# One written order for all engine queues, with batch 0's k and the whole of w_out loaded earlier

## The chip, the cores and the metric

The kernel runs on one core of one Trainium2 chip. The number given is device time in microseconds (us) of one execution; the reported time of a kernel is the median of its runs. The core has a matrix engine (PE, with its weight loads shown apart as PEld), a vector engine (DVE), an activation engine (ACT), a general engine (POOL), and a queue engine (SP) which here only issues transfers. POOL issues transfers too, and in the kernel before ACT issues one. Each engine works through its own queue strictly in program order; engines wait for each other by semaphores.

## The reference

Linear attention over 8 batches of 8 heads (576 positions, head size 64), and behind it a gated network without a nonlinearity:

```python
q_s = exp(q - max(q, axis=-1)); q_s = q_s / (sum(q_s, axis=-1) + 1e-9)   # over the 64 of a head
k_s = exp(k - max(k, axis=2));  k_s = k_s / (sum(k_s, axis=2) + 1e-9)    # over the 576 positions
kv  = einsum('bhsd,bhse->bhde', k_s, v)
attn = einsum('bhsd,bhde->bhse', q_s, kv)
x = attn.transpose(0, 2, 1, 3).reshape(4608, 512)
out = ((x @ w1) * (x @ w2)) @ w3 @ w_out        # w1, w2: 512x1024; w3: 1024x1024; w_out: 1024x512
```

All inputs and the output are float32. q, k and v have 1152 KB per batch each, w1, w2 and w_out 2 MB each, w3 4 MB: 38.8 MB are read.

## The kernel before, in words

The kernel is one class, `Plan` (L18), and one function. The function doesn't emit instructions as it goes: it registers **steps** with `plan.add` (L50): a name, an engine (or a choice of two, settled by the table `PICKS`, L206), an estimated length, a closure that emits the instructions, the steps it needs, and the ring of buffers that it takes from. At the end `plan.run` (L154) emits all 773 steps in one sequence, and that sequence is the order of every engine's queue. Before, `order` (L87) finds the sequence by list scheduling: it keeps a clock for each engine, takes the engine with the earliest start, and on it the ready step of highest worth, which is the longest path behind it (`tails`, L67) plus a lead from a table (`LEADS`, L166). For transfers it counts one bus of 409 GB/s.

The names, by stage:

- **Loads** (`load`, L396; table `LOADS`, L241). `q.0.1` is the second part of q of batch 0 (positions 4 to 8 of each group of 9; 640 KB), `q.0.0` the first (512 KB); `k.b`, `v.b`, `q.b` a whole batch. `w3.0` to `w3.3` are one row block of w3 each (512 KB of float32), `w3.4` and `w3.5` two (1 MB); `wo.0`, `wo.1` the halves of w_out (1 MB each); `w1.i`, `w2.i` column quarters (512 KB). Weights, and v of batches 0 and 1, are cast to float16 by the transfer. The weights and the first batches go through POOL's queue, at most eight in flight: the ninth waits for the first (the `slot` in L424). `q.0.1` is issued by SP, `q.0.0` by ACT. From `q.2` on loads go through SP, which starts on them once `LOADS[-3]` (L425) has landed.
- **Fold** (`fold`, L430): w3 and w_out are multiplied once into `W3O`. For each of 8 row blocks `ft`: `w3t.ft`, 8 transposes on PE (L434); `w3T.ft`, the copy out; `pf.ft.0` and `pf.ft.1`, 4 matmuls each (L444), which need `wo.0` and `wo.1`; `W3O.ft`, the scaled copy.
- **Attention** of batch b (L460): `qmx`, `qsub`, `qexp`, `qsm`, `qeps`, `qrc`, `qn` are the softmax of q (max, subtract, exp, sum, epsilon, reciprocal, product), for two parts `.0` and `.1`; `kmx`, `cb`, `ksub`, `kexp` the column maximum of k, its spread over partitions, subtract, exp; `vc` the cast of v from batch 2 on; `kv` (L555, L564) and `kv2` the product of k and v and its scaling; `qt`/`qT` the transposes of q for batches 0 and 1 on PE, and `qd` (L643) those of later batches as DMA transposes issued by SP; `xm`, `xt` (L661) the product with q and `xs`, `xts` its scaled copies.
- **Network** of chunk c (L772; 512 tokens of batch c, and a ninth chunk of the remainders): `up.1` and `up.0` (L786) with w2 and w1, `bs` the copy of the first, `ab` the product of the two on DVE (L801), `down.c.tb` with `W3O` (L808, in the last chunk L823), `os` the copy out, `st` the store.

PSUM rings hold 4 buffers for `up` and `w3t`, 2 for `down` and `pf`, 2 for the attention's products. Steps of POOL and DVE that read two tensors from SBUF (`port`, L159) are chained to one another by explicit waits in the early part, so that the two engines take turns.

Ahead of the first real matmul, 24 matmuls of zeros run on PE (`WARM`, L329, L363 to L368).

Of the kernel before, what the change touches and what calls it, by code (L numbers as in the profile page):

```python
# [10 lines left out]
F32 = mybir.dt.float32  # L11
# [6 lines left out]
class Plan:  # L18


    RATE = 409.0e3
    LAND = 1.7
    HOP = 0.15
    NEAR = 0.2
    LINKED = 50.0
    BUS = 2.2
    BEGIN = {"SP": 0.74, "POOL": 1.25, "DVE": 1.0, "ACT": 0.74, "PE": 1.0}

    def __init__(self, rings, leads, picks):
        self.rings = rings  # L30
        self.leads = leads
        self.picks = picks
        self.steps = {}

    @staticmethod
    def key(name):


        if name[0] == "up":
            return f"up{name[1]}_{min(name[2], 3)}"  # L40
        if len(name) > 2 and name[1] < 2 and name[0] not in ("bs", "ab", "down", "os", "st", "pf"):
            return "_".join(str(x) for x in name)
        return f"{name[0]}_{min(name[1], 3) if len(name) > 1 else 0}"

    @staticmethod
    def group(name):

        return f"{name[0]}_{min(name[1], 3)}_" + "_".join(str(x) for x in name[2:])
# [18 lines left out]
    def tails(self, users):  # L67
        tail = {}
        for first in self.steps:
            stack = [first]  # L70
            while stack:
                n = stack[-1]
                if n in tail:
                    stack.pop()
                    continue
                todo = [u for u, _ in users.get(n, ()) if u not in tail]
                if todo:
                    stack += todo
                    continue
                s = self.steps[n]  # L80
                own = s["length"] + (self.LAND + s["size"] / self.RATE if s["size"] else self.HOP)
                tail[n] = own + max([tail[u] if whole else tail[u] - own
                                     for u, whole in users.get(n, ())], default=0.0)
                stack.pop()
        return tail

    def order(self):  # L87
        steps = self.steps
        free = dict(self.BEGIN)
        ends = {}  # L90
        fifo = {tag: [] for tag in self.rings}
        given = {}
        users = {}
        for s in steps.values():
            for taken in s["gives"]:
                given.setdefault(taken, []).append(s["name"])
            s["open"] = len(s["needs"]) + len(s["after"])
            s["at"] = 0.0
            for n in s["needs"]:
                users.setdefault(n, []).append((s["name"], True))  # L100
            for n in s["after"]:
                users.setdefault(n, []).append((s["name"], False))
        tail = self.tails(users)
        for rank, n in enumerate(sorted(steps, key=str)):
            steps[n]["rank"] = -rank
        for s in steps.values():
            s["worth"] = tail[s["name"]] + s["lead"] + self.leads.get(self.key(s["name"]), 0.0)
        ready = [s for s in steps.values() if not s["open"]]
        bus = self.BUS
        port, holder = -9.0, None  # L110
        order = []
        while ready:
            could = {}
            for s in ready:
                at = max(free.get(s["eng"], 0.0), s["at"])
                if s["port"]:
                    at = max(at, port + (self.HOP if holder != s["eng"] else 0.0))
                if s["takes"]:
                    ring = fifo[s["takes"]]
                    last = [n for old in range(len(ring) - self.rings[s["takes"]],  # L120
                                               len(ring) - self.rings[s["takes"]] + s["slots"])
                            if old >= 0 for n in given.get(ring[old], ())]
                    if any(n not in ends for n in last):
                        continue
                    at = max([at] + [ends[n] + self.HOP for n in last])
                could.setdefault(s["eng"], []).append((at, s))
            assert could, "the plan is stuck"
            eng = min(sorted(could), key=lambda e: min(at for at, _ in could[e]))
            soon = min(at for at, _ in could[eng]) + self.NEAR
            at, s = max(((at, s) for at, s in could[eng] if at <= soon),  # L130
                        key=lambda c: (math.floor((c[1]["worth"] - c[0]) * 1e6 + 0.5), c[1]["rank"]))
            ready.remove(s)
            if s["takes"]:
                fifo[s["takes"]] += [s["name"]] * s["slots"]
            free[eng] = at + s["length"]
            if s["port"]:
                port, holder = at + s["length"], s["eng"]
            end = at + s["length"]
# [788 lines left out]
```

## Time and profile before

| | |
|---|---|
| median of 3 runs | 245.75 us (245.39, 245.75, 275.76) |
| the profiled execution | 246.01 us, of it 244.2 us from the first to the last instruction (the span) |
| PE busy | 234.2 us (96%) |
| DVE / ACT / POOL busy | 177.1 / 123.8 / 118.9 us |
| mean granted clock of PE | 0.993 |
| read / written | 38.80 MB / 9.44 MB |

The profile page gives busy times, the span in 40 slices, the chain of work that ended last, and groups of instructions with the idle time before them. The trace answers for a stretch of time with the instructions of an engine in order (the timeline), with who waited for whom (the waits) and with busy time and granted clock (the windows). A step can be found in it by its line and its tiles: L444 `po<-wosb,w3T` with four matmuls is one `pf`.

### The profile page before, as it was taken

Reading aid. Unit: us, or ns where it says so; the run is one execution under the profiler, and the core shown is the slowest. Engines: PE = TensorE matmul, PEld = TensorE weight load, DVE = VectorE, ACT = ScalarE, POOL = GpSimd, SP = SyncE. Lnnn points to the kernel's source line nnn. Section 1 sums busy time; section 2 is a strip of 40 time slices with the busy share of each in tenths; the row PEclk is TensorE's granted clock in tenths of the full one; section 3 lists DMA queues with packets and bytes.
Section 4 is the critical chain, followed back from the end, with each engine's and each line's share of the span. In section 5 each row is a group of like instructions: output and inputs, shape, how many; then the busy total and the mean of one; then the engine's idle time right before and its main releaser. Section 6 shows DMA issues by size and latency. Waiting matters only on the chain.

```text
span 244.2 us, 4819 instructions
## 1 busy us (share of the span) xinstructions
PE 234.2 (96%) x1908; PEld 114.8 (47%) x1908; DVE 177.1 (73%) x303; ACT 123.8 (51%) x189; POOL 118.9 (49%) x76
## 2 busy tenths in 40 slices
PE   7868999999999799999999999999999999999994
PEld 2435644556758244344444444444444344444443
DVE  0889789787998889998998899799965115573210
ACT  0556686466687357575565566555443612202221
POOL 8357769678880577086666646864470000000000
PEclk9979999999999999999999999999999999999999
DMA  7999999999999854986997299700840115000343
GB/s 206 267 253 252 305 300 200 249 369 387 392 399 209 215 120 148 397 190 76 348 313 148 51 364 319 160 4 6 183 83 3 43 43 132 0 0 0 86 132 129
DMA packets 37894, 45.66 MB, mean 187 GB/s; under 512 B 15984, under 2 KB 22384, under 8 KB 37872
## 3 DMA queue, kind: packets, MB, share of 16 engines
q1 hardware_dynamic: 29552, 33.69, 48.4%
q0 software_dynamic: 7792, 11.14, 20.7%
q10 hardware_dynamic: 528, 0.52, 0.6%
q8 instruction: 15, 0.25, 0.4%
q14 instruction: 7, 0.06, 0.1%
HBM read 38.80 MB, written 9.44 MB: 197 GB/s over the span
## 4 chain that ended last, share of the span: by engine, by line
PE 65%; DMA 21%; POOL 5%; DVE 4%; issue 2%; SPq 1%; ACT 1%; POOLq 0%; ACTq 0%
PE pab L786 40%; PE po L808 19%; DMA w<-in_moe_w_dram 6%; DMA w1sb<-in_moe_w_dram 5%; DMA v<-in_v_dram 4%; PE po L823 3%; DMA qT<-en 3%; DMA q<-in_q_dram 2%; POOL en L620 2%; POOL q L588 2%; PE xm L661 2%; PE pkv L555 1%; DVE q L588 1%; DVE qm L583 1%; DVE qr L601 1%
## 5 line engine op out<-in xcount | busy, mean ns | idle before, releaser
L801 DVE TENSOR_TENSOR ab<-pab,bsb 128x512 f16<-128x512 f32 x72 | 49.1, 686 | 28.7 <-PE pab L786 22.9
L786 PE MATMUL pab<-x,w2sb 128*128 128x512 f16 (+1 forms) x288 | 65.9, 356 | 0.0
L786 PE MATMUL pab<-x,w1sb 128*128 128x512 f16 (+1 forms) x288 | 65.9, 356 | 0.0
L808 PE MATMUL po<-W3O,ab 128*128 128x512 f16 x256 | 59.3, 380 | 0.0
L620 POOL TENSOR_TENSOR en<-eq,qr 128x1024 f16<-128x1024 f16 (+1 forms) x16 | 33.8, 2123 | 31.1 <-DVE qr L613 15.3
L342 ACT CAST bsb<-pab 128x512 f16<-128x512 f32 x42 | 24.5, 584 | 44.0 <-PE pab L786 34.6
L530 POOL TENSOR_TENSOR k<-k,cb 128x1152 f32<-128x1152 f32 x15 | 39.1, 2625 | 14.3 <-issue 7.1
L786 PEld LDWEIGHTS <-w2sb 128*128 128x128 f16 x320 | 30.6, 98 | 29.9 <-issue 0.2
L786 PEld LDWEIGHTS <-w1sb 128*128 128x128 f16 x320 | 30.7, 98 | 29.5 <-DMA w1sb<-in_moe_w_dram 0.2
L808 PEld LDWEIGHTS <-ab 128*128 128x128 f16 x256 | 23.9, 98 | 29.2 <-issue 2.9
L342 ACT COPY osb<-po 128x512 f32<-128x512 f32 (+1 forms) x33 | 19.1, 578 | 35.5 <-PE po L808 18.2
L588 POOL TENSOR_TENSOR q<-q,qm 128x1280 f32<-128x1280 f32 (+1 forms) x13 | 27.6, 2142 | 8.5 <-DVE qm L583 8.5
L342 DVE CAST bsb<-pab 128x512 f16<-128x512 f32 x30 | 20.4, 683 | 8.8 <-PE pab L786 7.8
L472 DVE TENSOR_REDUCE km<-k 128x128 f32<-128x1152 f32 x12 | 25.4, 2123 | 0.7 <-DMA k<-in_k_dram 0.7
L583 DVE TENSOR_REDUCE qm<-q 128x16 f32<-128x1024 f32 (+1 forms) x16 | 21.4, 1344 | 5.8 <-DMA q<-in_q_dram 5.8
L596 ACT ACTIVATE eq<-q 128x1024 f16<-128x1024 f32 (+1 forms) x16 | 18.6, 1164 | 7.3 <-POOL q L588 5.0
L601 DVE TENSOR_REDUCE qr<-eq 128x16 f32<-128x1024 f16 (+1 forms) x16 | 21.1, 1325 | 1.3 <-ACT eq L596 1.3
L538 ACT ACTIVATE ek<-k 128x1152 f16<-128x1152 f32 x16 | 18.6, 1165 | 5.9 <-POOL k L530 4.4
L346 ACT ACTIVATE x<-xm 128x512 f16<-128x512 f32 x29 | 16.2, 597 | 6.8 <-PE xm L661 6.7
L444 PE MATMUL po<-wosb,w3T 128*128 128x512 f16 x64 | 16.2, 394 | 3.0 <-ACT w3T L342 1.8
L342 ACT CAST v<-v 128x1152 f16<-128x1152 f32 x11 | 12.4, 1158 | 4.7 <-DMA v<-in_v_dram 4.7
L444 PEld LDWEIGHTS <-w3T 128*128 128x128 f16 x64 | 5.9, 100 | 10.0 <-ACT w3T L342 3.6
(62 smaller groups left out, 169.1 us busy)
## 6 DMA issues: line engine op xcount, KB each, us to landing
out_dram<-osb SPq DMA_DIRECT2D x66, 128.0 KB, 2.4
q<-in_q_dram SPq DMA_DIRECT2D x6, 1152.0 KB, 8.7
v<-in_v_dram SPq DMA_DIRECT2D x6, 1152.0 KB, 11.6
k<-in_k_dram SPq DMA_DIRECT2D x5, 1152.0 KB, 5.6
k<-in_k_dram POOLq DMA_DIRECT2D x3, 1152.0 KB, 11.9
v<-in_v_dram POOLq DMA_DIRECT2D x2, 576.0 KB, 14.6
w<-in_moe_w_dram POOLq DMA_DIRECT2D x2, 512.0 KB, 11.8
wosb<-in_moe_w_out_dram POOLq DMA_DIRECT2D x2, 512.0 KB, 11.8
```

The source lines that it names most:

```text
L342: return [(nc.scalar.copy if eng == "ACT" else engine[eng].tensor_copy)(out=out, in_=in_)]
L444: nc.tensor.matmul(st["pf", ft], lhsT=st["w3T", ft][:, gt, :], rhs=wosb[:, gt, :], start=(gt == 0), stop=(gt == N_FT - 1))
L472: dve.tensor_reduce(out=st["km", b][:, two(hp), :], in_=kb[:, two(hp), :, :].rearrange("p h j d -> p h d j"), axis=AX.X, op=ALU.max)
L530: return [engine[eng].tensor_tensor(out=kb[:, two(hp), :, :], in0=kb[:, two(hp), :, :], in1=st["cb", b][:, two(hp), None, :].broadcast_to( ...
L538: nc.scalar.activation(out=st["ek", b][:, hp, :, :].rearrange("p j (i d) -> p i j d", i=2), in_=kb[:, two(hp), :, :], func=AF.Exp)
L583: dve.tensor_reduce(out=st["qm", b][:, :, j], in_=qb[:, :, j, :], axis=AX.X, op=ALU.max)
L588: return [engine[eng].tensor_tensor(out=qb[:, :, j, :], in0=qb[:, :, j, :], in1=st["qm", b][:, :, j, None].broadcast_to([P, HH, n, D]), op ...
L601: dve.tensor_reduce(out=st["qr", b][:, :, slice(*PARTS[p])], in_=st["eq", b, p], axis=AX.X, op=ALU.add)
L620: return [engine[eng].tensor_tensor(out=st["en", b][:, j, :, :].rearrange("p j h d -> p h j d"), in0=st["eq", b, p], in1=st["qr", b][:, :, ...
L786: nc.tensor.matmul(st["p", one, c, sub, u][:, a * (t1 - t0):(a + 1) * (t1 - t0)], lhsT=w[:, ct, fb * P:(fb + 1) * P], rhs=x()[:, ct, t0:t1 ...
L801: dve.tensor_tensor(out=st["ab", c][:, nf * u:nf * u + nf, t0:t1], in0=cut(st["p", 0, c, sub, u]), in1=cut(st["bsb", c, sub, u]), op=ALU.mult)
L808: nc.tensor.matmul(st["po", c, tb], lhsT=st["ab", c][:, ft, tb * P:(tb + 1) * P], rhs=W3O[:, ft, :], start=(ft == 0), stop=(ft == N_FT - 1))
```

## The change

The list scheduler, its leads and its constants are removed. A string `ORDER` names all steps in sequence, and `run` emits them so, after asserting that each step's needs stand ahead of it. 76 steps move to another engine, nearly all by the table `PICKS`. Dead code goes (`PEMAX`, the 32-bit identity `ident32` on POOL); loads can be put on SP by a list `HW`, from which a path for uncast weights exists but is unused. In particular:

- `q.0.0` is issued by SP behind `q.0.1`, not by ACT.
- POOL's first loads come as w3.4, k.0, wo.0, wo.1, w3.3, w3.0, w3.1, where they were w3.4, wo.0, k.0, w3.3, wo.1, w3.0, w3.1; the identity is made ahead of w3.3, not behind q.1.0. Later, w3.2 is ahead of k.1 and w1.0 ahead of k.2.
- `LOADS[-3]`, which SP's `q.2` waits for, is now `w2.3`; before, it was `w1.3`.
- 17 zero matmuls at the start where there were 24, and 16 in the queue of PE right ahead of `pf.4.0`.
- The turn-taking waits cover the first 191 steps of the list; before, those planned for the first 50 us.
- The moves between engines: among them `qn.0.0` from POOL to DVE, `qsub.0.0` from DVE to POOL, the second `vc` of batches 2 to 7 from ACT to POOL, and 66 copies and epsilon steps (`bs`, `os`, `xs`, `xts`, `qT`, `W3O`, `w3T`, `qeps`) between ACT and DVE, in both directions.

PE's 243 steps are the same; their sequence differs in places. Up to `kv.0`, both sequences hold the same set. From `w3t.5` it now reads:

```text
w3t.5 w3t.4 (16 zeros) pf.4.0 pf.5.0 pf.4.1 qt.0.8 w3t.3 pf.5.1 qt.0.16 w3t.0 pf.3.0 pf.3.1 w3t.1
qt.0.0 pf.0.0 pf.1.0 pf.0.1 kv.0 ...
```

and before it was

```text
w3t.4 w3t.5 pf.4.0 pf.5.0 qt.0.0 w3t.3 pf.4.1 pf.5.1 w3t.0 qt.0.8 qt.0.16 pf.3.0 pf.3.1 w3t.1
pf.0.0 pf.0.1 pf.1.0 kv.0 ...
```

SP's queue around batch 2 is now `q.2 v.2 k.3 q.3 v.3 k.4 q.4 st.0.0 st.0.1 st.0.2 qd.2.1 qd.2.0 st.1.0 v.4`; before, `q.2 v.2 k.3 q.3 v.3 k.4 st.0.0 q.4 v.4 st.0.1 st.0.2 qd.2.1 qd.2.0`.

```diff
-    def order(self):
...
-        tail = self.tails(users)
...
-        return order, ends
-    def run(self, link):
-        held = None
-        for at, s in self.order()[0]:
+    def run(self, link, fill):
+        assert sorted(self.first, key=str) == sorted(self.steps, key=str)
...
+        for i, name in enumerate(self.first):
+            s = self.steps[name]
+            assert done.issuperset(s["needs"]) and done.issuperset(s["after"]), name
...
+            if ".".join(str(x) for x in name) in FILL:
+                fill(FILL[".".join(str(x) for x in name)])
             got = s["emit"]()
-            if s["port"] and at < self.LINKED:
+            if s["port"] and i < LINKED:
...
+LINKED = 191
+ORDER = """
+q.0.1 q.0.0 w3.4 k.0 wo.0 wo.1 ident w3.3 w3.0 qmx.0.1 w3.1 q.1.0 qsub.0.1 qexp.0.1 qmx.0.0 w3t.5
+v.0 w3t.4 qsm.0.1 w3T.4 qsub.0.0 qeps.0.1 w3.5 qexp.0.0 kmx.0.0 w3T.5 w3.2 pf.4.0 qrc.0.1 cb.0
+qn.0.1 pf.5.0 pf.4.1 qsm.0.0 k.1 qt.0.8 W3O.4 w2.0 w3t.3 qeps.0.0 ksub.0.1 pf.5.1 w3T.3 w1.0
+qt.0.16 w3t.0 qrc.0.0 qT.0.8 qn.0.0 pf.3.0 kexp.0.1 pf.3.1 w3T.0 ksub.0.0 w3t.1 W3O.5 qt.0.0
+w3T.1 W3O.3 pf.0.0 qmx.1.0 pf.1.0 kexp.0.0 qT.0.0 pf.0.1 qT.0.16 qsub.1.0 k.2 kv.0 w2.1 W3O.0
...
+ab.0.0.6 up.1.0.0.7 xs.1.0.1 ksub.2.1 xs.1.0.0 up.0.0.0.7 bs.0.0.7 qmx.1.1 kexp.2.0 up.1.1.0.0
+up.0.1.0.0 ab.0.0.7 qsub.1.1 kexp.2.1 up.1.1.0.1 qmx.2.1 bs.1.0.0 up.0.1.0.1 bs.1.0.1 ab.1.0.0
+down.0.0 qsub.2.1 qexp.1.1 qmx.2.0 vc.2.0 ab.1.0.1 q.3 up.1.1.0.2 v.3 qsm.1.1 vc.2.1 up.0.1.0.2
+k.4 qexp.2.1 up.1.1.0.3 qsub.2.0 os.0.0 qsm.2.1 up.0.1.0.3 qeps.1.1 bs.1.0.2 kv.2 qrc.1.1
+qexp.2.0 ab.1.0.2 down.0.1 qn.1.1 kv2.2 bs.1.0.3 q.4 st.0.0 ab.1.0.3 down.0.2 os.0.1 qmx.3.1
+st.0.1 qt.1.8 os.0.2 qeps.2.1 qrc.2.1 qt.1.16 qsub.3.1 down.0.3 qsm.2.0 qT.1.8 st.0.2 qT.1.16
+qmx.3.0 xm.1.1 down.1.0 xs.1.1.0 qn.2.1 kmx.3.1 xs.1.1.1 up.1.1.1.0 vc.3.0 qeps.2.0 up.0.1.1.0
+qexp.3.1 qd.2.1 qrc.2.0 kmx.3.0 qn.2.0 xt.1 up.1.1.1.1 os.0.3 up.0.1.1.1 bs.1.1.0 xts.1.0
+qsub.3.0 qd.2.0 up.1.1.1.2 xts.1.1 bs.1.1.1 qsm.3.1 ab.1.1.0 os.1.0 down.1.1 bs.1.1.2 ab.1.1.1
+st.1.0 up.0.1.1.2 os.1.1 qmx.4.1 up.1.1.1.3 v.4 st.1.1 ab.1.1.2 up.0.1.1.3 bs.1.1.3 qeps.3.1
+st.0.3 xm.2.0 vc.3.1 ab.1.1.3 down.1.2 xs.2.0.1 cb.3 xs.2.0.0 qsub.4.1 qexp.3.0 xm.2.1 down.1.3
...
+"""
+FILL = {
+    "begin": 17, "pf.4.0": 16,
 }
...
+HW = [
+    ("q", 0, 1), ("q", 0, 0),
+]
 LOADS = [
-    ("q", 0, 1), ("q", 0, 0), ("w3", 4), ("wo", 0), ("k", 0), ("w3", 3), ("wo", 1), ("w3", 0),
-    ("w3", 1), ("q", 1, 0), ("v", 0), ("w3", 5), ("k", 1), ("w3", 2), ("w2", 0), ("k", 2),
-    ("w1", 0), ("w2", 2), ("w2", 1), ("w1", 1), ("w1", 2), ("v", 1), ("w1", 3), ("w2", 3),
-    ("q", 1, 1),
+    ("w3", 4), ("k", 0), ("wo", 0), ("wo", 1), ("w3", 3), ("w3", 0), ("w3", 1), ("q", 1, 0),
+    ("v", 0), ("w3", 5), ("w3", 2), ("k", 1), ("w2", 0), ("w1", 0), ("k", 2), ("w2", 1),
+    ("w1", 1), ("w2", 2), ("w1", 2), ("v", 1), ("w2", 3), ("w1", 3), ("q", 1, 1),
 ]
...
-    if WARM:
-        zero = konst.tile([P, 512], F16)
-        dve.memset(zero, 0.0)
-        idle = p_att([P, 512], F32, "idle")
-        for i in range(WARM):
+    zero = konst.tile([P, 512], F16)
+    dve.memset(zero, 0.0)
+    def fill(n):
+        idle = p_o()
+        for i in range(n):
             nc.tensor.matmul(idle, lhsT=zero[:, 0:P], rhs=zero, start=True, stop=True)
+    if FILL.get("begin"):
+        fill(FILL["begin"])
...
-    loads = [(n, ("SP", "ACT")[i] if i < 2 and n[0] in ("q", "k") else "POOL")
-             for i, n in enumerate(LOADS)]
+    loads = [(n, "SP") for n in HW] + [(n, "POOL") for n in LOADS]
...
-    plan.run(link)
+    plan.run(link, fill)
```

## The prediction

> **What bounds the kernel now.** I read the page's head, then PE's waits, then PE's timeline of the first 30 us, then the chain around 70 us. The page:
>
> ```profile
> span 244.2 us, 4819 instructions
> PEclk9979999999999999999999999999999999999999
> DMA  7999999999999854986997299700840115000343
> ```
>
> PE's waits over the whole span, longest in total first (how long, how often, the longest):
>
> ```profile
> PE po L444 <- ACT w3T L342: 1.8, 1, 1.8
> PE idle L368 <- DVE zero L365: 1.6, 1, 1.6
> PE xm L661 <- DMA qT<-en: 1.3, 1, 1.3
> PE po L444 <- DMA wosb<-in_moe_w_out_dram: 1.3, 2, 1.0
> PE qtp L635 <- POOL en L620: 0.8, 1, 0.8
> ```
>
> That is all: one idle stretch at the first instruction, four before 22 us, one at `xm.2.0`. PE is the bound, and only what lies before its last stall can be gained. The stalls in PE's timeline (start, length, then the group; the bracket is the idle time before):
>
> ```profile
> 1.55 8.12 PE L368 MATMUL idle<-zero 128*128 128x512 f16 x24 [1.55 <-DVE zero L365]
> 11.65 1.02 PE L444 MATMUL po<-wosb,w3T 128*128 128x512 f16 x4 [0.98 <-DMA wosb<-in_moe_w_out_dram]
> 14.44 1.89 PE L444 MATMUL po<-wosb,w3T 128*128 128x512 f16 x4 [1.77 <-ACT w3T L342]
> 18.11 1.89 PE L444 MATMUL po<-wosb,w3T 128*128 128x512 f16 x8 [0.28 <-DMA wosb<-in_moe_w_out_dram]
> 21.32 0.73 PE L635 MATMUL qtp<-ident,en 128*128 128x128 f16 x10 [0.83 <-POOL en L620]
> 26.80 0.48 PE L555 MATMUL pkv<-v,ek 64*64 64x64 f16 x36
> ...
> 81.17 0.41 PE L661 MATMUL xm<-qT,kv 64*64 64x512 f16 x4 [1.30 <-DMA qT<-en]
> ```
>
> From 21.32 PE is full except for the 1.30 us ahead of `xm.2.0`, at 81.17, until 240.97; then copy, store and end, 3.2 us. The chain shows what `xm.2.0` waited for (start, length, what):
>
> ```profile
> 66.58 1.91 POOL en L620
> 68.49 4.18 POOL q L588 x2
> 72.67 1.99 SPq L643
> ...
> 74.76 6.36 DMA qT<-en
> 81.12 0.04 issue
> 81.17 0.41 PE xm L661 x4
> ```
>
> `qn.2.0` ended at 68.5, but its transpose landed only at 81.1.
>
> **The floor.** PE's real work: 218.3 us after 21.32 (240.97 - 21.32 - 1.30), and before it 0.48 for each of four `w3t` and of `qt.0.0` and 0.86 for each of four `pf` at full clock, 5.9; together 224.2. No `pf` can run before `wo.0`, nor can any order change that sum. This is why a gain over 2% (4.9 us, about what a measurement of this kernel can tell from no change) isn't in reach: with `wo.0` at 14.65 (below) and two `w3t` done, 14.65 - 0.96 + 224.2 + 3.2 = 241.1 is the least span, 3.1 below today's.
>
> **Term 1: the head, to `kv.0`.** The loads first. In the trace w3.4 lands at 9.36 (POOL's queue waits for it until then) and w3.2 at 31.66, with 9.31 MB read between them: 0.417 MB/us. By that rate wo.0 would land at 11.87 and wo.1 at 18.5; PE's waits end at 11.65 and 18.11. So landings are the running sum of the list. New list: w3.4 9.36, k.0 12.15, wo.0 14.65, wo.1 17.2, w3.3 18.4, w3.0 19.7, w3.1 21.0, v.0 25.05, w3.5 27.55, w3.2 28.8, k.1 31.65, w2.0 32.9, w1.0 34.2. One SP queue for q instead of two may shift the first by a us; q.0.0 has until 9.4.
>
> PE's queue: 17 zeros end near 8.0, the two `w3t` follow 9.36, the 16 zeros run to 13.8 if at full clock (0.21 each), `pf.4.0` and `pf.5.0` from 14.65 to 16.4, then from 17.2 without a gap if all inputs are there: seven `pf` halves, three `w3t` and 18 transposes of q, 8.55 us by the paces above (0.86 for 4 matmuls, 0.48 for 8 transposes): `kv.0` at 25.75.
>
> The vector side: before, `kmx.0` started at 15.91 and `kv.0` at 26.80. New, from k.0 at 12.15: `kmx.0` 2.87, `qrc.0.1` 0.28, `cb.0` 2.28, `qsm.0.0` 1.21, `qeps` 0.18, `ksub.0.1` 1.36, `qrc.0.0` 0.25, `qn.0.0`, on DVE now (no row; 1.2 as its float32 subtract of that size, between 0.7 as the float16 copy and 1.9 as on POOL), `ksub.0.0` on POOL 2.63, `kexp.0.0` 1.16, handoffs 0.3: 13.7, so 25.9. The earlier k is mostly spent on q's steps put between. Ahead of it, `qsm.0.1` ends by 12.2 unless the 1.28 us table load of ACT, which today starts when ACT's own q lands, comes behind `qsub.0.1`; then 1.2 later. I take 0: ACT idles until 9.4.
>
> Both give about 25.9, a gain of 0.9, with margins of 0.1 to 0.8 at w3.3, w3.0 and `qn.0.0`. Bounds: from 1.1 gained (PE's own 25.75) to 1.1 lost (the table load, and 0.8 of such margins overrun).
>
> **Term 2: 26 to 81 us.** PE's set between `kv.0` and `xm.2.0` is the same: 79.87 - 26.80 = 53.1 us, so it arrives there at 79.0. Covers: w2.1 lands at 38.3 and is wanted at 39.3, w1.3 47.4 and 48.7, k.1's `qn.1.0` 36.9 and 37.9. About 1 us each; every us beyond costs a us.
>
> When do the transposes of batch 2 land? The DVE queue from `qmx.1.1` (50.2, when q.1.1 lands) to `qrc.2.0` sums to 19.0 by the rows, plus waits of 1.1 for q.2 and about 1 at `qsm.2.1`, which waits for `qexp.2.1` behind v's cast on ACT (v.2 landed at 58.05): 71.4. `qn.2.0` 1.91: 73.3, 4.8 later than today. SP's issue 1.38 and the flight. Flight today is 6.36 and the issue 4.16: eight loads of 1152 KB stand ahead in SP's queue, and the transfers move 396 GB/s until 72. New, v.4 stands behind, which frees 2.8 us by the rate, and `qn.2.0` comes later. So nearer the median flight of all twelve, 3.5: 78.2; with 6.36, 81.1. I take 79.7, the middle, just over PE's 79.0: 1.5 earlier than 81.17.
>
> **Term 3: the rest.** PE was full from 81.17 to the end, and the set is the same: 0. Cover for the moved copies: ACT is 51% busy; `vc` on POOL adds 1.15 to about 13.7 us per batch, against 22.7 per chunk on PE. For batch 3, `qn.3` now follows both `ksub.3`; POOL's rows put its end at 92.2 and, with issue and flight, the landing at 97.1, against 99.0 when PE gets there (19.3 after `xm.2.0`, as today): cover 2. The last 26 steps of PE and SP are identical: tail 0. The first zero matmul still waits for DVE at 1.55. ident32's 0.6 us of POOL at 6.86 was hidden.
>
> **Sum.** 244.2 - 1.5 = 242.7 span; the profiled execution 246.01 - 1.5 = 244.5. It stood 0.26 over the median, so 244.25; I say **244.3**, -0.6%.
>
> **Rivals.**
>
> *A, the zeros meet a halved clock.* After its idle stretches at 10.7 and 12.7 the granted clock was 0.51 at 14 to 15 and 0.50 until 17, and back at 1 by 18. The new gap of 1.3 us ahead of w3.4 could do it sooner: zeros took 0.43 each in the first 5.5 us, so 16 last 6.9, from 10.4 to 17.3, and the two `pf` of wo.0 come after, 1.9 late: `kv.0` 27.7, `xm.2.0` 80.8, 0.4 gained: 245.4. For: about as much PE work (1.9 us) lies between 7.1 and 10.5 as before the drop. Against: 0.9 of it is dense. Chance 0.18.
>
> By the Trainium skill, TensorE: Matmul & The Clock Gate, Part 1, activity is judged over free-running windows of about 3.4 us, and Part 4 says that transposes don't count as PE work; the rise at 7.08 and 17.3 in the trace, three windows apart, agrees. By that rule A would be the likelier on some runs and not on others, as the phase falls; the sum would be 245.4.
>
> *B, the stall stays.* Transposes fly 6.4 us again: 81.1, nothing gained: 245.7. Speaks for it: stores and five loads still share that queue. Chance 0.17.
>
> *C, slower: batch 2's chain slips.* Place: ACT's queue, where `vc.2.0` waits for v.2 with `qexp.2.1`, `os.0.0`, `bs.1.0.2`, `qexp.2.0` and `bs.1.0.3` behind it, and DVE's, where `qrc.2.0` waits behind two maxima of q.3 and one of k.3. A us of v.2, q.3 or k.3 then is a us of `qn.2.0`. It decides from `qn.2.0` at 76.3 with the short flight (3 late), or 73.4 with the long one; with 5 late and the long one `xm.2.0` starts at 86.1, 4.9 later than today: 250.7. Spoken against: today's v.2 leaves room, and k.3 is ahead of q.3. Chance 0.18, half of it past 2%.
>
> *D, the list doesn't do what it says*: what arrives when doesn't follow the list, and the head stays as it is: 245.75. The fit of wo.0 and wo.1 nearly excludes it: 0.02.
>
> The forecast, 243.4 to 245.2, has 0.45. The range begins at 242.6, the floor in this measure (245.75 - 3.1), and ends at 250, which leaves out about 0.12, the longer half of C and a stall that I don't see after 82 (0.03 of the forecast's). Slower by 2% (over 250.7) 0.11, of the same two; faster by 2% 0.01, landings quicker than the rate; the rest, 0.88, is within 2%.
>
> **What would show it.** Right: `pf.4.0` at 14.6, the second half of w_out at 17.2, `kv.0` near 25.9, no idle from 17 on but under a us in all; `xm.2.0` between 79 and 80.5; PE's end near 239.5. Term 1 wrong: waits at L444 or L635 behind DVE. A: zeros 0.43 apart after 10. B and C: a wait at L661 of 2 us and more, with POOL's `en` ending before or after 74. The prediction fails most if a stall opens after 82, where there is none to judge from.

## The result and the profile after

The changed kernel takes **243.5 us** in the median (243.27 to 243.72, 4 runs) against 245.69 for the kernel before in the same runs: ratio **0.9921, 95% interval 0.9906 to 0.9937**. The ratio leaves out the one execution of 275.76. That is a gain of 0.8%: small, but the interval ends well short of 1. It is within the 2% that the forecast had, and 0.8 us below its 244.3.

In what follows line numbers differ between kernels, since each has its own file: in the changed one a `pf` is L427, `xm` L621, `kv` L515, `qt` L595, `w3t` L415, the zeros L325, `up` L735, `down` L757 and, in the last chunk, L772.

The page of the changed kernel:

```profile
span 241.5 us, 4827 instructions
PE 234.5 (97%) x1917; PEld 114.6 (47%) x1917; DVE 170.8 (71%) x293; ACT 123.4 (51%) x194; POOL 124.0 (51%) x79
PEclk9999999999999999999999999999999999999999
DMA  6999999999999808992897999701750215000343
```

The profiled execution took 243.27 us, the median less 0.2; its span is 2.7 below that of before. PE's busy time has not shrunk (234.2 then, 234.5 now), but 10.0 us of it are zeros now (33 matmuls) and 8.1 were then (24), so the real work takes some 1.6 us less. The dip of the clock in the third slice, which made it longer, is gone. PE's waits, in total, times, longest:

```profile
PE po L325 <- DVE zero L320: 1.6, 1, 1.6
PE po L427 <- DMA wosb<-in_moe_w_out_dram: 1.2, 2, 0.8
PE w3t L415 <- DMA w<-in_moe_w_dram: 0.8, 1, 0.8
PE pkv L515 <- DMA v<-in_v_dram: 0.2, 1, 0.2
```

No wait for a copy, none for `qn`, none at `xm`; behind the first zeros, what is left are landings before 26 us. PE's timeline (start, length, group; in brackets the idle time before it):

```profile
8.73 1.21 PE L415 MATMUL w3t<-ident,w 128*128 128x128 f16 x16 [0.83 <-DMA w<-in_moe_w_dram]
9.78 3.62 PE L325 MATMUL po<-zero 128*128 128x512 f16 x16
14.14 1.89 PE L427 MATMUL po<-wosb,w3T 128*128 128x512 f16 x8 [0.75 <-DMA wosb<-in_moe_w_out_dram]
16.48 1.02 PE L427 MATMUL po<-wosb,w3T 128*128 128x512 f16 x4 [0.45 <-DMA wosb<-in_moe_w_out_dram]
...
25.32 0.48 PE L515 MATMUL pkv<-v,ek 64*64 64x64 f16 x36 [0.16 <-DMA v<-in_v_dram]
...
78.45 0.41 PE L621 MATMUL xm<-qT,kv 64*64 64x512 f16 x4
```

The lines to compare are those of `kv.0` and `xm.2.0`. `kv.0` started at 26.80 and starts at 25.32; `xm.2.0` at 81.17 behind 1.30 of waiting, now at 78.45 behind none. From `xm.2.0` to PE's end it was 159.76 (240.93 - 81.17) and is 159.76 (238.21 - 78.45). So the 2.7 us of the profiled executions are 1.48 in the head and 1.24 between `kv.0` and `xm.2.0` (54.37 down to 53.13), nothing behind. The medians differ by 2.2 only, because the execution shown of before lies 0.3 above its median and the one shown of the changed kernel 0.2 below. Some of that is in the head of before: in two runs below that leave that head as it was (e6 and e8) `kv.0` came at 26.53 and 26.51, so the execution that was shown of before was some 0.3 late there.

SP's queue around that place shows why `xm.2.0` doesn't wait. First before, then in the changed kernel (SP's rows are the issuing of a transfer, not the transfer):

```profile
62.38 0.53 SPq L400 DMA_DIRECT2D q<-in_q_dram  x1
62.96 1.56 SPq L400 DMA_DIRECT2D v<-in_v_dram  x1
64.62 5.77 SPq L834 DMA_DIRECT2D out_dram<-osb  x4
70.50 7.35 SPq L643 DMA_TRANSPOSE qT<-en  x2
```

```profile
61.90 0.37 SPq L377 DMA_DIRECT2D q<-in_q_dram  x1
62.32 4.50 SPq L783 DMA_DIRECT2D out_dram<-osb  x6
69.48 5.22 SPq L603 DMA_TRANSPOSE qT<-en  x2
74.79 1.81 SPq L783 DMA_DIRECT2D out_dram<-osb  x2
76.66 0.59 SPq L377 DMA_DIRECT2D v<-in_v_dram  x1
```

The 1152 KB of v.4 are issued only after both transposes. `qn.2.0` on POOL ended at 72.33, 3.8 later than before (68.5), and still its transpose, issued at 72.61, landed at 78.00, 3.1 earlier than before (81.1). That is 0.4 ahead of PE.

### The profile page after: what moved, and what is told of

Same layout as the page of the kernel before. It is cut to its first block, busy times and chain, and to the rows that moved or that the text cites. A ratio compares the mean times of both kernels' runs of the same rounds, so it can differ in the third digit from the quotient of the medians.

```text
span 241.5 us, 4827 instructions
## 1 busy us (share of the span) xinstructions
PE 234.5 (97%) x1917; PEld 114.6 (47%) x1917; DVE 170.8 (71%) x293; ACT 123.4 (51%) x194; POOL 124.0 (51%) x79
## 4 chain that ended last, share of the span: by engine, by line
PE 88%; DMA 7%; POOL 2%; issue 1%; ACT 0%; POOLq 0%
PE pab L735 52%; PE po L757 23%; DMA v<-in_v_dram 7%; PE po L772 3%; PE po L427 3%; PE pkv L515 2%; PE xm L621 2%; POOL w L377 1%; PE w3t L415 1%; PE xt L621 1%; PE pkv L524 1%; POOL wosb L377 0%; PE qtp L595 0%; POOL q L377 0%; POOL k L377 0%
## 5 line engine op out<-in xcount | busy, mean ns | idle before, releaser
L735 PE MATMUL pab<-x,w1sb 128*128 128x512 f16 (+1 forms) x288 | 65.9, 356 | 0.0
L735 PE MATMUL pab<-x,w2sb 128*128 128x512 f16 (+1 forms) x288 | 65.8, 356 | 0.0
L298 ACT CAST bsb<-pab 128x512 f16<-128x512 f32 x59 | 34.6, 586 | 52.0 <-PE pab L735 51.7
L757 PE MATMUL po<-W3O,ab 128*128 128x512 f16 x256 | 59.5, 380 | 0.0
L735 PEld LDWEIGHTS <-w2sb 128*128 128x128 f16 x320 | 30.7, 98 | 30.6 <-issue 0.2
L735 PEld LDWEIGHTS <-w1sb 128*128 128x128 f16 x320 | 30.6, 98 | 29.6 <-issue 0.2
L580 POOL TENSOR_TENSOR en<-eq,qr 128x1280 f16<-128x1280 f16 (+1 forms) x15 | 32.1, 2141 | 15.3 <-ACT x L302 6.3
L757 PEld LDWEIGHTS <-ab 128*128 128x128 f16 x256 | 24.0, 98 | 29.2 <-issue 2.7
L548 POOL TENSOR_TENSOR q<-q,qm 128x1024 f32<-128x1024 f32 (+1 forms) x14 | 29.7, 2126 | 8.6 <-DVE qm L543 6.3
L298 ACT COPY osb<-po 128x512 f32<-128x512 f32 (+1 forms) x29 | 16.6, 572 | 28.5 <-PE po L757 22.6
L543 DVE TENSOR_REDUCE qm<-q 128x20 f32<-128x1280 f32 (+1 forms) x16 | 21.4, 1344 | 4.1 <-DMA q<-in_q_dram 4.1
L561 DVE TENSOR_REDUCE qr<-eq 128x20 f32<-128x1280 f16 (+1 forms) x16 | 21.3, 1330 | 0.4 <-ACT eq L556 0.4
L556 ACT ACTIVATE eq<-q 128x1280 f16<-128x1280 f32 (+1 forms) x16 | 18.6, 1165 | 5.6 <-POOL q L548 2.9
L498 ACT ACTIVATE ek<-k 128x1152 f16<-128x1152 f32 x16 | 18.5, 1164 | 2.5 <-POOL k L490 2.5
L298 DVE CAST bsb<-pab 128x512 f16<-128x512 f32 x13 | 9.0, 690 | 13.4 <-PE pab L735 13.3
L427 PE MATMUL po<-wosb,w3T 128*128 128x512 f16 x64 | 15.3, 379 | 1.2 <-DMA wosb<-in_moe_w_out_dram 1.2
L325 PE MATMUL po<-zero 128*128 128x512 f16 x33 | 10.0, 470 | 1.6 <-DVE zero L320 1.6
L427 PEld LDWEIGHTS <-w3T 128*128 128x128 f16 x64 | 5.8, 98 | 7.8 <-ACT w3T L298 1.2
## 6 DMA issues: line engine op xcount, KB each, us to landing
wosb<-in_moe_w_out_dram POOLq DMA_DIRECT2D x2, 512.0 KB, 12.1
```

What stands on the lines that cost most here:

```text
L298: return [(nc.scalar.copy if eng == "ACT" else engine[eng].tensor_copy)(out=out, in_=in_)]
L427: nc.tensor.matmul(st["pf", ft], lhsT=st["w3T", ft][:, gt, :], rhs=wosb[:, gt, :], start=(gt == 0), stop=(gt == N_FT - 1))
L543: dve.tensor_reduce(out=st["qm", b][:, :, j], in_=qb[:, :, j, :], axis=AX.X, op=ALU.max)
L548: return [engine[eng].tensor_tensor(out=qb[:, :, j, :], in0=qb[:, :, j, :], in1=st["qm", b][:, :, j, None].broadcast_to([P, HH, n, D]), op ...
L556: nc.scalar.activation(out=st["eq", b, p], in_=qb[:, :, j, :], func=AF.Exp)
L561: dve.tensor_reduce(out=st["qr", b][:, :, slice(*PARTS[p])], in_=st["eq", b, p], axis=AX.X, op=ALU.add)
```

## The experiments

Twelve kernels ran, each compared with the kernel before on the same chip. All compute the whole reference. The last two columns are starts in us in the profiled execution.

| kernel | median us | kernel before there | ratio, 95% interval | `kv.0` | `xm.2.0` (wait) |
|---|---|---|---|---|---|
| changed | 243.50 | 245.69 | 0.9921 (0.9906 to 0.9937) | 25.32 | 78.45 (0) |
| e1, changed without zeros in the wait | 244.39 | 245.29 | 0.9960 (0.9940 to 0.9979) | 26.87 | 79.85 (0) |
| e2, changed with the old first loads | 247.18 | 245.29 | 1.0063 (1.0037 to 1.0089) | 28.29 | 81.27 (0) |
| e13, e2 with zeros in its new gap | 246.02 | 245.38 | 1.0017 (1.0003 to 1.0031) | 27.81 | 80.80 (0) |
| e3, changed with q.0.0 issued by ACT | 243.54 | 245.29 | 0.9911 (0.9887 to 0.9934) | 25.60 | 78.73 (0) |
| e4, changed with v.4 ahead | 244.67 | 245.29 | 0.9971 (0.9953 to 0.9989) | 25.56 | 80.10 (1.29) |
| e11, changed with `pf.4.1` later | 244.58 | 245.38 | 0.9957 (0.9944 to 0.9971) | 26.45 | 79.42 (0) |
| e5, before with zeros | 245.22 | 245.20 | 1.0001 (0.9991 to 1.0011) | 26.46 | 80.37 (0.72) |
| e7, before with the new first loads | 245.25 | 245.20 | 0.9996 (0.9982 to 1.0009) | 27.12 | 80.57 (0.27) |
| e9, before with both | 245.57 | 245.51 | 0.9998 (0.9984 to 1.0013) | 26.57 | 80.53 (0.69) |
| e6, before with v.4 behind | 249.96 | 245.20 | 1.0200 (1.0164 to 1.0237) | 26.53 | 79.64 (0) |
| e8, e6 with two casts later | 244.60 | 245.36 | 0.9972 (0.9961 to 0.9984) | 26.51 | 79.52 (0) |
| e10, e8 with new loads and zeros | 244.52 | 245.51 | 0.9972 (0.9961 to 0.9982) | 26.54 | 79.61 (0) |

### The zeros: e1

```diff
 FILL = {
-    "begin": 17, "pf.4.0": 16,
+    "begin": 17,
 }
```

> The changed kernel without the 16 zeros ahead of pf.4.0; all else as it is. PE then has nothing from 9.8 to 14.1 us. Theory 1 (the zeros hold the granted clock): the clock is halved from about 14 to 17.4, as it was in the kernel before after its own idle stretch; the two pf halves at 14.1 take 3.4 us instead of 1.7, pf.4.1 follows at 17.6 instead of 16.5, PE arrives at kv.0 1.1 us late, at 26.4, and the time is 244.6 (1.1 over the changed kernel's 243.5). Theory 2 (the zeros are not needed): the clock stays or the lost time is hidden behind v.0, which lands at 25.2: kv.0 at 25.3, 243.5.

PE's timeline of e1, and then its windows (busy time per engine; the first of the last three columns is the granted clock):

```profile
14.15 5.12 PE L427 MATMUL po<-wosb,w3T 128*128 128x512 f16 x12 [4.10 <-DMA wosb<-in_moe_w_out_dram]
```

```profile
14.00:16.00 2.00, 1.84 (x5) 0.69 (x5) 1.88 (x7) 0.00 (x0) 1.52 (x2) 0.50 1.02 205
16.00:18.00 2.00, 2.00 (x7) 0.64 (x5) 1.90 (x6) 0.00 (x0) 2.00 (x2) 0.50 1.12 209
```

Twelve matmuls take 5.12 where the same number elsewhere in the head takes 2.75: behind 4.1 us without work the clock stands at 0.50. Theory 1 holds, and more strongly than it had it: `kv.0` at 26.87, not 26.4. In the changed kernel the zeros fill that gap and the clock stays at 1.00 in every window of the head; in all 23 executions of the changed kernel, e3, e4 and e11, which have these zeros, the mean clock was 0.998 or more. Without them the kernel gives back 0.9 us of the median (243.50 to 244.39, across two comparisons), and 1.4 in the profiled executions.

The Trainium skill (TensorE: Matmul & The Clock Gate, Part 1) has it that the clock halves after an idle window of about 3.4 us whose phase is free. A gap of 4.10 ahead of 5 us of half clock agrees with that in kind. But the granted clock of e1 was already 0.67 on average from 12.0 to 12.5 and 0.50 behind that, little over 2 us after PE's last transpose (10.05), and in e2, next, a gap of 2.63 was enough. So here less than 3.4 us without any matmul sufficed.

### The loads: e2 and e13

```diff
-q.0.1 q.0.0 w3.4 k.0 wo.0 wo.1 ident w3.3 w3.0 qmx.0.1 w3.1 q.1.0 ...
+q.0.1 q.0.0 w3.4 wo.0 k.0 w3.3 ident wo.1 w3.0 qmx.0.1 w3.1 q.1.0 ...
...
-    ("w3", 4), ("k", 0), ("wo", 0), ("wo", 1), ("w3", 3), ("w3", 0), ("w3", 1), ...
+    ("w3", 4), ("wo", 0), ("k", 0), ("w3", 3), ("wo", 1), ("w3", 0), ("w3", 1), ...
```

> The changed kernel with the first seven of POOL's loads in the order of before (w3.4, wo.0, k.0, w3.3, wo.1, w3.0, w3.1); every other queue as changed. Theory 1 (kv.0 is set by the vector chain behind k.0, and the loads land as the running sum of the list): k.0 lands at 14.3 instead of 11.75, kv.0 starts 2.5 later at 27.8, PE waits there about 1.5 to 2.5, and the time is 245.5 to 246: the list without its loads gains nothing over before. Theory 2 (the gain comes from the order of the engines' queues and not from the loads): kv.0 by 25.8, 243.5 to 244.

It came out slower than any theory had it: 3.7 us over the changed kernel, with a spread of 2.9 us (246.13 to 249.03). PE's timeline and a window of its fastest execution:

```profile
13.46 1.89 PE L427 MATMUL po<-wosb,w3T 128*128 128x512 f16 x8
17.98 1.86 PE L427 MATMUL po<-wosb,w3T 128*128 128x512 f16 x4 [2.63 <-DMA wosb<-in_moe_w_out_dram]
```

```profile
18.00:20.00 2.00, 1.88 (x5) 0.42 (x5) 1.86 (x8) 0.12 (x1) 2.00 (x2) 0.50 1.10 247
```

With wo.1 behind k.0 and w3.3, `pf.4.1` waits until 17.98, and here too the idle stretch is paid a second time, in half clock. k.0 is late as well: `kmx.0` starts at 14.43 instead of 11.79. The mean clock was 0.986 in three of the ten executions (247.43, 248.18 and 249.03 us) and 0.991 to 0.993 in the seven others (246.13 to 247.49). To tell the clock from the later landings, e13 adds zeros in that gap:

```diff
-    "begin": 17, "pf.4.0": 16,
+    "begin": 17, "pf.4.0": 16, "pf.4.1": 12,
...
-        idle = p_o()
+        idle = p_att([P, 512], F32, "idle")
```

> The changed kernel with the old order of the first seven loads, as run once, and 12 more matmuls of zeros ahead of pf.4.1, where that run idled 2.63 and then worked at a granted clock of 0.50 from 18 to 20 (all zeros go to a PSUM buffer of the attention's ring, which is free then). Theory 1 (that halved clock is what it lost beyond the later loads): pf.4.1 still starts at 18.0, the clock stays at 1, kv.0 starts at 27.6 to 27.8, when kexp.0.0 is done, 0.5 to 0.7 earlier than in that run; the time is 245.3 to 245.7 with little spread, near the kernel before. Theory 2 (the excess has another cause): kv.0 at 28.2 and more, 246 to 247.5 with a spread over 1 us, as in that run.

PE's timeline of e13:

```profile
15.21 2.75 PE L325 MATMUL idle<-zero 128*128 128x512 f16 x12
18.00 1.02 PE L427 MATMUL po<-wosb,w3T 128*128 128x512 f16 x4
...
27.81 0.48 PE L515 MATMUL pkv<-v,ek 64*64 64x64 f16 x36
```

`pf.4.1` starts where it did and takes 1.02 instead of 1.86; the clock is 1 throughout. `kv.0` comes 0.48 sooner, the median falls by 1.2 and the spread to 0.84. So the half clock is part of e2's excess, and probably most of its spread; what e2's slower executions looked like was not seen. The median is above the 245.3 to 245.7 expected. The profiled execution (246.27) lost 0.54 more at 143.5, where PE waited for a transpose of a later batch; whether the five executions below 245.9 lack that wait isn't known. With the clock held, the old order of loads costs 2.5 us in the changed kernel (246.02 against 243.50), of which 0.54 in the profiled execution is that later wait.

### q.0.0 from ACT: e3

```diff
-    loads = [(n, "SP") for n in HW] + [(n, "POOL") for n in LOADS]
+    loads = [(n, ("SP", "ACT")[i]) for i, n in enumerate(HW)] + [(n, "POOL") for n in LOADS]
```

> The changed kernel with q.0.0 issued by ACT again. Asks why the first w3 rows landed at 8.7 where 9.36 was forecast. Theory 1 (two hardware queues with q take a larger share from POOL's queue than one): w3.4 lands at 9.3, q.0.0 before 7 instead of near 7.9, k.0 and the w_out halves as now because the sum of bytes is the same; the time 243.5, within 0.3. Theory 2 (the first landing moved for another reason): w3.4 at 8.7 still.

The time is that of the changed kernel. `w3t.5` starts at 8.83 behind w3.4, so the sooner landing in the changed kernel doesn't come from q.0.0's queue; that theory falls. The other runs say what it was: POOL's wait for w3.4 ended at 9.00 in e5, 9.14 in e9, 9.51 in e7 and 9.54 in e8, all with the old queues for q, at 9.36 in before and at 8.97 to 9.21 in the changed kernel, e1, e2 and e3. The difference of 0.4 lies within what one execution and the next differ by.

### v.4 ahead of the transposes: e4

```diff
-... bs.1.0.3 q.4 st.0.0 ab.1.0.3 ...
+... bs.1.0.3 q.4 v.4 st.0.0 ab.1.0.3 ...
-... up.1.1.1.3 v.4 st.1.1 ab.1.1.2 ...
+... up.1.1.1.3 st.1.1 ab.1.1.2 ...
```

> The changed kernel with v.4 ahead of the stores and transposes of batch 2 in SP's queue, as before. Theory 1 (the transposes wait behind the bytes queued ahead of them): 1152 KB at 0.417 MB/us is 2.8 us, so qd.2.0 lands at 80.9 instead of 78.05, PE waits at xm.2.0 for 2.4 us, and the time is 245.9. Theory 2 (qn.2.0's end at 72.3 and SP's own issue set the landing): xm.2.0 at 78.5 as now, 243.5.

PE's timeline of e4 at `xm.2.0`:

```profile
80.10 0.41 PE L621 MATMUL xm<-qT,kv 64*64 64x512 f16 x4 [1.29 <-DMA qT<-en]
```

The stall is back, as long as before (1.30), and the kernel gives back 1.2 us, half of the 2.4 that theory 1 had. The transpose landed at 80.06 instead of 78.00: 2.1 later, of the 2.8 that the 1152 KB would take at the head's 0.417 MB/us. By the Trainium skill (DMA: Bandwidth & Descriptors, Queues, rings and completion order) a queue's descriptors are taken in ring order on each DMA engine, and SP has one such row; that fits a transpose that comes after bytes issued ahead of it. In this trace they land in that order: q.4 at 73.12, v.4 at 76.02, the last store at 77.97, the two transposes at 79.17 and 80.06.

The delay isn't a longer flight, though, but a later issue. SP's queue in e4:

```profile
62.32 0.70 SPq L377 DMA_DIRECT2D v<-in_v_dram  x1
63.07 7.53 SPq L783 DMA_DIRECT2D out_dram<-osb  x6
73.18 4.88 SPq L603 DMA_TRANSPOSE qT<-en  x2
```

`qn.2.0` ended at 72.61, 0.28 later than in the changed kernel, but its transpose was issued at 76.08, 3.47 later; from issue to landing it then took 3.98 where the changed kernel took 5.39. What SP waited for shows in the times of the landings. In every one of the fourteen traces no transfer of SP is issued before the one eight places ahead in its queue has landed. Eight ahead of the second transpose stands q.4 in the changed kernel (landed at 72.55, transpose issued at 72.61) and v.4 in e4 (76.02 and 76.08). So v.4 costs a transpose behind it one of eight places as well as the time of its bytes; how much is due to which was not separated.

### v.4 behind them, in the kernel before: e6 and e8

```diff
-        for at, s in self.order()[0]:
+        order = self.order()[0]
+        names = [s["name"] for at, s in order]
+        one = order.pop(names.index(("v", 4)))
+        order.insert(names.index(("qd", 2, 0)), one)
+        for at, s in order:
```

> The kernel before with one step moved: v.4 behind qd.2.0 in SP's queue. Theory 1 (bytes queued ahead held the transposes): qd.2.0 lands 2.8 earlier, at 78.3, the wait of 1.3 at xm.2.0 goes, 244.4. Theory 2 (it was POOL or SP's issue): no change, 245.7. A part of theory 1 that could fail: v.4 is then late for vc.4 and PE waits at kv.4.

This miss taught most. `xm.2.0` indeed came at 79.64 without a wait. But the kernel is 2.0% slower (1.6 to 2.4). First ACT's timeline of e6, then PE's:

```profile
80.58 1.16 ACT L346 CAST v<-v 128x1152 f16<-128x1152 f32 x1 [5.67 <-DMA v<-in_v_dram]
81.64 0.58 ACT L346 CAST bsb<-pab 128x512 f16<-128x512 f32 x1
```

```profile
79.98 1.04 PE L812 MATMUL po<-W3O,ab 128*128 128x512 f16 x4
83.66 1.20 PE L812 MATMUL po<-W3O,ab 128*128 128x512 f16 x4 [2.63 <-DVE ab L805]
...
85.81 3.50 PE L812 MATMUL po<-W3O,ab 128*128 128x512 f16 x8
```

ACT reached `vc.4.0` at 74.9 and stood there for 5.67 us, until v.4 had landed. Behind it in ACT's queue were a `bs` and a `qeps`; DVE stood 5.44 us at the reciprocal that follows `qeps`, with `ab` behind it, and PE's `down` waited 2.63 for `ab`. Then the clock was down to 0.50 from 86 to 88, so that eight matmuls took 3.50 instead of 1.90. In the changed kernel the same move has the casts moved too: `vc.4.0` comes later in ACT's queue. e8 does just that in the kernel before:

```diff
...
+        for name, ahead in ((("v", 4), ("qd", 2, 0)), (("vc", 4, 0), ("os", 1, 3)),
+                            (("vc", 4, 1), ("bs", 2, 0, 1))):
+            one = order.pop([s["name"] for at, s in order].index(name))
+            order.insert([s["name"] for at, s in order].index(ahead) + 1, one)
...
```

> The kernel before, with v.4 moved on SP's list behind both of batch 2's transposes, and batch 4's two casts of v later in ACT's list as well (vc.4.0 after os.1.3, vc.4.1 after bs.2.0.1), as the list of the changed kernel has them. Theory 1 (the transposes were late because of the bytes of v.4 queued ahead of them; the run that moved v.4 alone lost only because ACT stood at vc.4.0 until v.4 had landed): xm.2.0 starts at 79.6 to 79.9 without a wait for the transposes, ACT has no wait for v.4 over 1 us between 70 and 90, and the time is 244.0 to 244.6, 0.7 to 1.3 under the kernel before; the head stays at 26.8. Theory 2 (v.4 so late costs elsewhere too, in the casts or in kv.4): xm.2.0 comes earlier all the same, but a new wait of PE over 0.5 us appears behind it and the time is 245.2 or more.

PE's timeline of e8:

```profile
79.52 0.41 PE L665 MATMUL xm<-qT,kv 64*64 64x512 f16 x4
79.86 1.90 PE L812 MATMUL po<-W3O,ab 128*128 128x512 f16 x8
```

No wait at `xm.2.0`, none behind it, and 244.6: the step that was a 2% loss alone is a gain of 0.7 us (0.8 between the medians) once the consumer is moved along. In e8 the second transpose was issued at 71.08 and landed at 75.99 (74.76 and 81.12 before). Of the parts of the change that were run by themselves this is the only one that gains.

### Loads and zeros in the kernel before: e5, e7, e9, e10

```diff
 e5:
+            self.zeros(s["name"])
             got = s["emit"]()
...
+        n = {("pf", 4, 0): 4, ("pf", 5, 0): 8}.get(name, 0)
...
 e7:
+        new = [("w3", 4), ("k", 0), ("wo", 0), ("wo", 1), ("w3", 3), ("w3", 0), ("w3", 1)]
+        places = [i for i, (at, s) in enumerate(order) if s["name"] in new]
+        for i, name in zip(places, new):
+            order[i] = (order[i][0], self.steps[name])
...
```

> The kernel before with zeros added in its waits alone: 4 ahead of pf.4.0 and 8 ahead of pf.5.0. Theory 1 (the clock is held, but the next landings set the pace): granted clock 1 from 12 to 18, pf.5.0 in 0.9 instead of 1.7 us, but pf.4.1 still waits for wo.1 at 18.1 and the second q transpose for qn.0.1 at 21.3: kv.0 at 26.8, 245.7, no gain. Theory 2 (the halved clock was on the path): about 0.9 to 1.3 gained, 244.5 to 244.8.

> The kernel before with only its first seven loads on POOL in the new order (w3.4, k.0, wo.0, wo.1, w3.3, w3.0, w3.1). Theory 1 (an earlier k is of no use while DVE does q's steps first, and wo.0 comes later): kmx.0 still starts at 15.9, pf.4.0 at 14.1 instead of 11.65, kv.0 between 26.8 and 27.5, time 245.7 to 246.4. Theory 2 (the loads alone make the gain): kv.0 by 25.8, 244.7.

Neither moves the time. With zeros alone PE is early, but waits 1.03 for wo.1 and 0.87 for `qn`. With the loads alone PE idles 4.09 ahead of wo.0 and eight matmuls take 3.57 at half clock; `kv.0` is later than before (27.12). The 11.8 that is given for k.0's landing below is the changed kernel's; with the loads alone it was 12.20.

e9 takes both together (16 zeros, ahead of `pf.4.0`), e10 adds the move of v.4 and its casts:

> The kernel before with the new order of the first seven loads and 16 matmuls of zeros ahead of pf.4.0; the list scheduler's order of all engines stays, and v.4 stays ahead of batch 2's transposes. Theory 1 (these two parts together make the new head): kv.0 starts at 25.3 to 25.6, as in the changed kernel. Theory 2 (the vector engines' order of batch 0 is the other half: with the loads alone kmx.0 started only at 15.56, behind two sums and a subtract of q, though k.0 had landed at 11.8, and kexp.0.0 ended at 26.2): the clock stays at 1, PE is early, but waits for kexp.0.0, kv.0 starts at 26.2 to 26.5. By both the time hardly moves, since what the head gains turns into a wait at xm.2.0 for the transposes behind v.4: 244.7 to 245.2.

> The same, and v.4 behind batch 2's transposes with batch 4's two casts later on ACT: all three parts, on the order of the kernel before. Theory 1 (they are the whole gain): kv.0 at 25.3 to 25.6, xm.2.0 at 78.4 to 78.8, time 243.4 to 243.8. Theory 2 (the head needs the vector engines' new order as well): kv.0 at 26.2 to 26.5, xm.2.0 at 79.3 to 79.5, time 244.2 to 244.6, no more than the run with v.4 and the casts alone.

PE's timeline of e10:

```profile
14.19 1.89 PE L453 MATMUL po<-wosb,w3T 128*128 128x512 f16 x8
15.92 0.61 PE L644 MATMUL qtp<-ident,en 128*128 128x128 f16 x8
17.87 0.71 PE L443 MATMUL w3t<-ident,w 128*128 128x128 f16 x8 [1.34 <-DMA w<-in_moe_w_dram]
18.42 1.89 PE L453 MATMUL po<-wosb,w3T 128*128 128x512 f16 x8
...
26.54 0.48 PE L564 MATMUL pkv<-v,ek 64*64 64x64 f16 x36
```

The second theory holds nearly to its numbers: `kv.0` at 26.57 and 26.54 (26.2 to 26.5 were expected), e10 at 244.52, no better than e8. e9's time, 245.57, is above the 244.7 to 245.2 that both theories had: PE waits 0.69 at `xm.2.0` for the transposes. In one point that theory was wrong: PE isn't early. Its old sequence has `w3t.3` directly behind `qt.0.0`, so it waits 1.34 for w3.3 and leaves wo.1, which is there by 16.9 (POOL's wait for it ends then), unused until 18.42. DVE's timeline of the same kernel has the other half:

```profile
15.29 0.28 DVE L622 RECIPROCAL qr<-qr 128x20 f32<-128x20 f32 x1 [0.38 <-ACT qr L616]
15.66 1.23 DVE L490 TENSOR_TENSOR kmx<-k 128x1024 f32<-128x1024 f32 x1
```

k.0 has been there since 12.1 at the latest (POOL's wait again), but DVE reaches `kmx.0` only at 15.66 (11.79 in the changed kernel), and `kexp.0.0` ends at 26.33, 0.2 ahead of `kv.0`. So by this trace both queues have to change for `kv.0` to move by more than 0.2. PE's new sequence on the old order of the vector engines was not run; e11 is near the reverse of it.

### One step of PE's sequence moved back: e11

```diff
-... pf.5.0 pf.4.1 qsm.0.0 k.1 qt.0.8 W3O.4 w2.0 w3t.3 qeps.0.0 ksub.0.1 pf.5.1 w3T.3 w1.0
+... pf.5.0 qsm.0.0 k.1 qt.0.8 w2.0 w3t.3 pf.4.1 qeps.0.0 ksub.0.1 pf.5.1 w3T.3 W3O.4 w1.0
```

> The changed kernel with one step of PE's queue moved back to where the kernel before has it, behind the first transposes of q and w3t.3: pf.4.0, pf.5.0, qt.0.8, w3t.3, pf.4.1 (W3O.4 behind w3T.3 accordingly). Theory 1 (PE's sequence, not only the vector engines' chain, sets kv.0): PE idles from 15.9 until the product qn.0.1 ends, at 17.3, or w3.3 lands, pf.4.1's 0.86 come after that, and kv.0 starts at 26.0 to 26.5, the time is 244.1 to 244.7. Theory 2 (kv.0 waits for v.0 and kexp.0.0 anyway, PE's sequence is free): kv.0 at 25.3 to 25.5, time 243.4 to 243.7.

PE's timeline of e11:

```profile
17.45 0.62 PE L595 MATMUL qtp<-ident,en 128*128 128x128 f16 x8 [1.27 <-POOL en L580]
...
26.45 0.48 PE L515 MATMUL pkv<-v,ek 64*64 64x64 f16 x36
```

One step of 0.86 us, no longer there to fill the wait for `qn.0.1`, costs 1.13 at `kv.0` and 0.9 to 1.1 us of the time (by the ratios or by the medians). The kernel before, given the loads and the zeros, stood at the same 26.5.

## Why the prediction was right, and where it was off

**What bounds the kernel, and the floor**: right. PE was the bound before and is now, only the two places named gave anything, and the span is 241.5 against a floor put at 241.1. That floor was counted from a wo.0 at 14.65; PE had it by 14.14, with which the same sum gives 240.6. One side remark was wrong: that a measurement can't tell less than 2% from no change. The interval here is 0.3% wide.

**Term 1, the head**: the mechanism was right, its size was not: 0.9 forecast, 1.48 measured in the profiled executions, of which some 0.3 is the late `kv.0` of the one before. Both lines of the sum were too long, by 0.6 and 0.95. *PE's line*: wo.0 and wo.1 were put at 14.65 and 17.2 by the running sum at 0.417 MB/us and `pf` started behind them at 14.14 and 16.48. For these two the rate was right, the start of the sum was not: 9.36 is when POOL's wait for w3.4 ended, and w3.4 had landed at 9.07 by the trace before and at 8.69 in the changed kernel. From 8.69 the same sum gives 13.98 for wo.0, which landed at 14.01. The trace before had a hint of it: the sum gave 11.87 and 18.5 where PE's waits ended at 11.65 and 18.11. From 16.48 PE then did work that the forecast put at 8.55 in 8.68, without a gap, to 25.16. *The vector line*: `kmx.0` started at 11.79, not 12.15, and the chain to the end of `kexp.0.0` took 13.16 (24.95 - 11.79), not 13.7. v.0, forecast for 25.05, landed at 25.19 and became the last: `kv.0` waited 0.16 for it, to 25.32. That agreement is luck, since a sum from 8.69 puts it at 24.4, and over the runs it landed anywhere from 24.42 (e1) to 25.65 (e13). That the table load of ACT would cost nothing held (at 5.03, long before it matters). "The earlier k is mostly spent on q's steps put between" held as well. That k and the whole of w_out come sooner was only part of the cause, though, and the prediction didn't separate the parts: the same loads with the same zeros, on the old queues of PE and DVE, gave `kv.0` 26.54 (e10), and one `pf` half put back costs 1.13 (e11). The steps that I listed one by one were the right ones; their order, not the landings alone, made the gain.

**Term 2, to `xm.2.0`**: PE's set was put at 53.1 us and took 53.13. The transposes were put at 79.7, the middle between 78.2 and 81.1; they landed at 78.00, just under the lower end. The middle was not what was wrong: the flight was 5.39, a little over the middle of 3.5 and 6.36. Two other pieces of that sum were too long. `qn.2.0` ended at 72.33 and not 73.3; and SP's issue of 1.38 was counted twice, because the flight in the profile runs from the start of the issue: only 0.28 lay between `qn.2.0`'s end and the issue at 72.61. So PE was not held, and `xm.2.0` came at 78.45. The picture of eight loads ahead in SP's queue was wrong too: when the transposes were issued before, at 70.50, six of them had landed (k.4 at 69.92), and only q.4, v.4 and stores were under way. What held the transposes in e4 is the transfer eight places ahead; why issuing the first of them took 4.16 in the kernel before is not shown.

**Term 3, the rest at nothing**: 159.76 and 159.76. Right, tail included.

**The sum** was 1.5 where 2.7 came in the profiled executions and 2.2 in the medians: of the 1.2 in the profiled executions 0.58 are term 1's, since PE arrived at 79.0 less 0.58, and 0.7 are the transposes', which were put at 79.7, 0.7 above PE's arrival, and held nothing.

**Rival A** (zeros at half clock) did not happen: 16 zeros took 3.62 us. But what it priced is real: without the zeros the half clock comes (e1), for 0.9 us of the median, near the 1.1 that A took off the gain. **Rival B** did not happen; e4 makes it happen with one step of SP's queue. **Rival C** did not happen: `vc.2.0` waited 0.49 for v.2, and though `qn.2.0` came 3.8 us later than before, its transposes were there 0.4 ahead of PE. Its mechanism, ACT's queue standing at a cast whose v is not there, was what made e6 4.8 us slower; that the prediction's price for it was 4.9 is chance, since that was worked out for batch 2's chain. The prediction had not seen that the same queue waits for v.4 itself, which the change moves: it was kept harmless by moving `vc.4`. **D** is excluded by e2 and e4, which undo single entries of the list and lose what they bought.

**What each part is worth.** Moving v.4 with its casts is worth 0.7 to 0.8 alone. Loads, zeros, or both, on the old order, are worth nothing: `kv.0` stays at 26.5 and later, and PE waits for the transposes at `xm.2.0` anyway (0.27 to 0.72). Taken away from the changed kernel, the zeros cost 0.9, the place of v.4 1.2, one `pf` half 1.1, the order of the loads 2.5 with the clock held: 5.7 in sum, out of a gain of 2.2. So they aren't parts to be added: in the head each is worth something only with the others. What e10 lacks to the changed kernel, 1.0 to 1.2 us, is the order of PE's and the vector engines' queues, the moves between engines and the turn-taking waits; of these only one step of PE's order was run apart (e11), and which of the others the head needs stays open. Behind `kv.0` they gain PE nothing: its 53.1 us to `xm.2.0` and 159.76 from there are those of before. No version faster than the changed kernel came out: e3 is its equal, and what PE still waits for is the landing of w3.4, wo.0, wo.1 and v.0.

## What to carry to other kernels

Moving a load back in a queue moves its consumer's wait with it: look for the instruction that waits for it on an in-order engine and put that one later too, or the gain at one place returns as a stall at another, here of 2%. An earlier landing is worth something only if the queues behind it are reordered to use it, so price a change of loads by the order of the engines that consume them. And fill an idle stretch of the matrix engine that can't be removed, since here, behind a stretch of 4.1 us, 12 matmuls took 5.12 us at half clock and not 2.75.

## What the runs showed of the hardware that was not expected

- A halved clock made stalls of under 3 us longer. In e2 2.63 idle were followed by a clock of 0.50; ten executions spread over 2.9 us, and over 0.84 with zeros in that gap (e13). In e6 2.63 idle at 81 were followed by 0.50 from 86 to 88. But e8 idled 1.33, 1.31 and 1.50 in its head and its mean clock was 0.998.
- In none of the fourteen traces was a transfer of SP issued before the one eight places ahead of it had landed. v.4 ahead of a transpose delayed its issue by 3.47 us, up to v.4's own landing, and its landing by 2.1 (e4).
- The first landing of POOL's queue scatters by half a microsecond: w3.4, issued at 1.24 or 1.25 in each of the fourteen kernels, landed between 8.69 and 9.25, and POOL's wait for it ended some 0.3 later. A forecast of landings from one trace can't be better than that. Of the 0.64 that term 1 missed by at wo.0's landing (14.65 and 14.01), 0.38 is this scatter and 0.29 the wait of POOL taken for the landing.
